# k^T v per head in two column tiles instead of per pair of heads, in one fused attention and MLP kernel

## The chip, the cores and the metric

The kernel runs on one core of one Trainium2 chip. Each core has a matrix engine (TensorE, PE in the profile, with its weight loads as PEld), three engines for elementwise work (VectorE: DVE, ScalarE: ACT, GpSimd: POOL) and a queue that issues the transfers (SyncE: SP). The metric is the time of one execution on the device in microseconds; lower is better.

## The reference

Two layers follow each other. The first is linear attention with a norm per head; the second is a token mix of low rank and an MLP in float32:

```python
# q, k, v: (8 batches, 8 heads, 576 tokens, 64)
kv  = einsum('bhsd,bhse->bhde', k, v)           # per head: 64 x 64, summed over 576 tokens
out = einsum('bhsd,bhde->bhse', q, kv)
x   = out / sqrt(mean(out*out, -1) + 1e-6) * g_norm   # heads side by side: (8, 576, 512)
u   = x + (x^T @ U @ V)^T                       # U: 576 x 32, V: 32 x 576
y   = u + maximum(u @ w_ch1, 0) @ w_ch2         # 512 -> 2048 -> 512
```

The change concerns the first line, `kv`, for batches 2 to 7.

## The kernel before

**Tiling.** Heads are taken in pairs, so that 2 x 64 columns fill the 128 columns of the matrix engine: four pairs a batch, and a *kv step* for each pair (`kv_step`). Tokens are the summed dimension: 576 = 4 chunks of 128 and a tail of 64. A pair's k and v come in one tile `kv_sb` (128 x 1024: four chunks of k, then four of v, `load_kv`) and the tail in `kvt_sb`.

**What a kv step makes.** The product of a pair's k and v is 128 x 128, of which only the two 64 x 64 blocks on the diagonal are wanted (each head with itself). They go into a tile `kvb` whose other blocks stay zero; there are two such tiles, in turn. The out step (L284, L286) then multiplies q by this `kvb`.

**float32 and float32r.** A matmul with float32 operands stands in the profile as two records (a weight load and a matmul each); one with float32r operands (rounded to fewer bits) as one. Where float32r is used, values are split into a high part and the rest, and the products are summed. The constant `NATIVE = 2` says that batches 0 and 1 do without such splits. In batches 2 to 7, the four main chunks of k^T v are float32 (L261, 128 x 128 columns). The tail is made from a split: it is loaded twice, into both halves of 128 partitions; ACT rounds it to float32r (L256), DVE takes the rest (L257 for k, L258 for v) in a tile `tails`, and one float32r matmul of 256 columns (L259) gives the products of k with the high part of v and with its rest, side by side. DVE adds these two sides when it moves the result to `kvb` (L272, twice, for each head).

**What sets the order.** The MLP runs over nine blocks of 512 tokens and, in each, over 16 slices of the hidden dimension: L432 to L434 (first weights, 12 matmuls of 512 columns a slice), relu and split on ACT and DVE (L441, L442), then L449 (second weights, 12 matmuls of 512 columns). The attention of the next batch is cut into steps that the code hands out between the slices (`prep_schedule`): kv, out, t (the product with U, L354 and L356; in batches 0 and 1 L350) and mix (L424). A scheduler with a timeline of its own orders each engine's instructions within that; so parts of one step can come to stand apart. Results wait in banks of PSUM, three of them for the steps (`pp`). `kv_sb` and `kvt_sb` have one buffer each: the next load waits until the last reader of the one before is done.

Of the kernel before, what the change touches and what calls it, by code (L numbers as in the profile page):

```python
# [10 lines left out]
F32 = mybir.dt.float32  # L11
F32R = mybir.dt.float32r
# [4 lines left out]
ALU = mybir.AluOpType  # L17
AX = mybir.AxisListType

B, H, S, D = 8, 8, 576, 64  # L20
DM, DF, R = 512, 2048, 32
P = 128
NPAIR = H // 2
NT = 5
MAIN = 4 * P
TAIL = S - MAIN
# [8 lines left out]
NATIVE = 2  # L35
# [24 lines left out]
def build(ctx: ExitStack, tc: tile.TileContext, kv_in, kvt0_in, kvt_in, q_in, uv_in, g_in, w_in, out):  # L60
    nc = tc.nc
# [5 lines left out]
    sc = ctx.enter_context(tc.tile_pool(name="sc", bufs=1))  # L67
# [71 lines left out]
    def move(which, n, out, in_, mul=None):  # L139

        e = ENG[which][n]
        if e == "a":
            if mul is None:
                nc.scalar.copy(out=out, in_=in_)
            else:
                nc.scalar.mul(out=out, in_=in_, mul=mul)
        else:
            eng = nc.vector if e == "v" else nc.gpsimd
            if mul is None:
                eng.tensor_copy(out=out, in_=in_)  # L150
            else:
                eng.tensor_scalar(out=out, in0=in_, scalar1=mul, scalar2=None, op0=ALU.mult)
# [88 lines left out]
    def bank():  # L241
        bank_no[0] += 1
        if startup[0] and bank_no[0] % (7 - NEARLY) >= 3 - NEARLY:
            return ps_y.tile([P, 512], F32, name="y")
        return ps_p.tile([P, 512], F32, name="pp")

    def kv_step(b, p):


        m = loads.pop(("kv", b, p))  # L250
        t = loads.pop(("t", b, p))
        pp = bank()
        kb = kvb[p % 2]
        if b >= NATIVE:
            both = sc.tile([P, 3 * P], F32R, name="tails")
            nc.scalar.copy(out=both[:, 0:2 * P], in_=t)  # L256
            nc.vector.tensor_tensor(out=both[TAIL:, 0:P], in0=t[TAIL:, 0:P], in1=both[TAIL:, 0:P].bitcast(F32), op=ALU.subtract)  # L257
            nc.vector.tensor_tensor(out=both[:, 2 * P:], in0=t[:, P:], in1=both[:, P:2 * P].bitcast(F32), op=ALU.subtract)  # L258
            nc.tensor.matmul(pp[:, 0:2 * P], lhsT=both[:, 0:P], rhs=both[:, P:], start=True, stop=False)  # L259
        for i in range(4):  # L260
            nc.tensor.matmul(pp[:, 0:P], lhsT=m[:, i * P:(i + 1) * P], rhs=m[:, MAIN + i * P:MAIN + (i + 1) * P],  # L261
                             start=(i == 0 and b < NATIVE), stop=(i == 3 and b >= NATIVE))
        if b < NATIVE:
            lo = TAIL * (p % 2)
            nc.tensor.matmul(pp[:, 0:P], lhsT=t[lo:lo + TAIL, 0:P], rhs=t[lo:lo + TAIL, P:2 * P], start=False, stop=True)
        parts = pp[:, 0:2 * P].rearrange("p (s c) -> p c s", s=2)
        for lo in (0, D):
            own = slice(lo, lo + D)
            if b < NATIVE:
                move("kv", p if b == 0 else -1, kb[own, own], pp[own, own])  # L270
            else:
                nc.vector.tensor_reduce(out=kb[own, own], in_=parts[own, own], axis=AX.X, op=ALU.add)  # L272

    state = {}

# [289 lines left out]
    def spread_v(n, eng):  # L565
        for k in range(4):
# [3 lines left out]
        out=uv, in_=uvraw.bitcast(U32).rearrange("p (n t) -> p n t", t=2)[:, :, 1].bitcast(F32), func=AF.Abs)  # L570
# [8 lines left out]
                                                  op=ALU.subtract)  # L579
# [94 lines left out]
    def prep_schedule(b):  # L674
# [8 lines left out]
        if b < B:  # L683
            for p in range(NPAIR):
                steps = STEPS0 if b == 1 else STEPS
                base = steps["gap"] * p

                def kv(p=p):
                    kv_step(b, p)
                    nxt = (b, p + 1) if p + 1 < NPAIR else (b + 1, 0)  # L690
                    if nxt[0] < B:
                        load_kv(*nxt)

                def o(p=p):
                    for what in (out_step, stats_step, mul_step, xsplit_step, turn_step):
                        what(b, p)
                    nxt = (b, p + 1) if p + 1 < NPAIR else (b + 1, 0)
                    if nxt[0] < B:
                        load_q(*nxt)

                def t(p=p):
                    t_step(b, p)
                    t4_step(b, p)

                for at, what in (("kv", kv), ("out", o), ("t", t), ("mix", lambda p=p: mix_step(b, p))):
                    todo.setdefault(base + steps[at], []).append(what)
# [108 lines left out]
```

## Time and profile before

| what | value |
|---|---|
| runs shown | 924.99, 926.73, 927.0 us; median 926.73 |
| span of the profiled execution | 924.0 us |
| records of L261 (four chunks, 28 steps) | 224 |
| records of L259 (tails, 24 steps) | 24 |
| median time from issue to landing of `kvt_sb` loads in batches 2 to 7 | 3.2 us |

The span runs from the first to the last instruction of one execution; the page gives no time of that execution beside it. In rows of groups, the columns are line, engine, operation, what it writes and reads, the shape (rows * weight columns, then partitions x moving columns), the count, busy time in us, mean duration of one in ns, idle time before it and what ended that. Matmul records overlap, and their ends are modelled, so starts say more than durations; the chain in order of time gives each piece from the end of the piece before it.

### The profile page before, as it was taken

What the parts mean: (1) busy time and instruction counts of PE and PEld (TensorE: products, weight loads), DVE (VectorE), ACT (ScalarE), POOL (GpSimd) and SP (SyncE); (2) the same over time, 40 slices, a digit from 0 to 9 for tenths busy, and PEclk for the clock granted to TensorE, in tenths of its full rate; (3) what the DMA queues carried; (4) which work ended last, traced back from release to release, by engine and by line L of the source; (5) the groups of instructions that cost most, each with busy time, mean ns of one, the idle gap of its engine ahead of it and who ended that gap; (6) DMA issues with size and microseconds to landing.
All of it is one profiled execution on the core that took longest, in us unless ns stands there. A gap on an engine that the chain in (4) does not pass through costs nothing.

```text
span 924.0 us, 12146 instructions
## 1 busy us (share of the span) xinstructions
PE 910.9 (99%) x4548; PEld 761.0 (82%) x4548; DVE 402.2 (44%) x870; ACT 271.4 (29%) x572; POOL 47.8 (5%) x61
## 2 busy tenths in 40 slices
PE   8899999999999999999999999999999999999998
PEld 7678888888878888888888888888788888888887
DVE  5799974534444435434344445434334231112112
ACT  5677742322222223222222223222222121111110
POOL 2000002000110002000200010000200020002000
PEclk9999999999999999999999999999999999999999
DMA  9952223211121112212121121212111010001001
GB/s 342 416 206 71 93 63 100 87 32 58 51 79 55 48 57 95 58 31 77 51 60 55 55 68 56 80 32 71 58 49 27 14 46 1 1 0 46 1 1 46
DMA packets 43019, 65.48 MB, mean 71 GB/s; under 512 B 9680, under 2 KB 27856, under 8 KB 42960
## 3 DMA queue, kind: packets, MB, share of 16 engines
q1 hardware_dynamic: 42960, 64.70, 21.2%
q8 instruction: 36, 0.59, 0.3%
q14 instruction: 23, 0.19, 0.1%
HBM read 46.97 MB, written 9.44 MB: 61 GB/s over the span
## 4 chain that ended last, share of the span: by engine, by line
PE 86%; DVE 6%; DMA 3%; ACT 2%; SPq 2%; issue 1%; POOL 0%; DVEq 0%; POOLq 0%; ACTq 0%
PE y L449 37%; PE h L432 13%; PE h L433 13%; PE h L434 13%; PE pp L261 2%; PE pp L284 2%; SPq L343 2%; DVE dec L127 1%; DVE st L460 1%; DMA kvq<-kv_in 1%; ACT top L131 1%; DMA out<-st 1%; DVE hl L442 1%; PE pp L354 1%; PE pp L424 1%
## 5 line engine op out<-in xcount | busy, mean ns | idle before, releaser
L449 PE MATMUL y<-hh,ws 128*128 128x512 f32 x1000 | 328.1, 394 | 0.0
L442 DVE SCALAR_TENSOR_TENSOR hl<-h,hh 128x512 fp32r<-128x512 f32 x143 | 98.4, 688 | 319.1 <-ACT hh L441 317.8
L449 PEld LDWEIGHTS y<-hh,ws 128*128 128x128 f32 x1000 | 181.0, 189 | 33.1 <-issue 0.2
L441 ACT ACTIVATE hh<-h 128x512 fp32r<-128x512 f32 x143 | 85.4, 597 | 404.0 <-PE h L434 404.0
L432 PE MATMUL h<-uth,ws 128*128 128x512 f32 x500 | 197.5, 395 | 2.2 <-DVE hl L442 2.2
L433 PE MATMUL h<-utl,ws 128*128 128x512 f32 x500 | 195.4, 391 | 0.0
L434 PE MATMUL h<-uth,ws 128*128 128x512 f32 x500 | 195.1, 390 | 0.0
L449 PE MATMUL y<-hl,ws 128*128 128x512 f32 x500 | 193.6, 387 | 0.0
L432 PEld LDWEIGHTS h<-uth,ws 128*128 128x128 f32 x500 | 93.9, 188 | 24.9 <-DVE hl L442 4.3
L434 PEld LDWEIGHTS h<-uth,ws 128*128 128x128 f32 x500 | 93.9, 188 | 20.2
L449 PEld LDWEIGHTS y<-hl,ws 128*128 128x128 f32 x500 | 93.9, 188 | 19.2
L433 PEld LDWEIGHTS h<-utl,ws 128*128 128x128 f32 x500 | 94.0, 188 | 18.4
L461 POOL TENSOR_TENSOR st<-st,utl 128x512 f32<-128x512 f32 x32 | 41.1, 1308 | 782.6 <-DVE st L460 781.0
L449 PE MATMUL y<-hh,w2s 128*128 128x512 f32 (+1 forms) x144 | 48.1, 396 | 2.8 <-ACT hh L441 2.7
L426 DVE TENSOR_TENSOR ut<-pp,ut 128x288 f32<-128x288 f32 x56 | 25.0, 455 | 43.5 <-DMA ut<-xt 30.3
L389 ACT ACTIVATE uth<-ut,g_sb 128x448 fp32r<-128x448 f32 (+7 forms) x56 | 27.6, 530 | 47.7 <-DVE ut L426 26.5
L460 DVE TENSOR_TENSOR st<-y,uth 128x512 f32<-128x512 f32 x32 | 21.4, 686 | 41.7 <-PE y L449 29.1
L449 PEld LDWEIGHTS y<-hh,w2s 128*128 128x128 f32 x144 | 26.6, 188 | 10.1 <-ACT hh L441 4.6
L390 DVE SCALAR_TENSOR_TENSOR utl<-ut,g_sb,uth 128x448 fp32r<-128x448 f32 (+7 forms) x56 | 26.9, 513 | 14.3 <-ACT uth L389 7.7
L300 DVE TENSOR_REDUCE sums<-x 128x10 f32<-128x640 f32 x28 | 22.9, 817 | 21.0 <-ACT x L288 20.9
L261 PE MATMUL pp<-kv_sb 128*128 128x128 f32 x224 | 30.3, 275 | 0.0
L284 PE MATMUL pp<-kvb,q_sb 128*128 128x128 f32 x224 | 29.5, 275 | 0.0
(188 smaller groups left out, 858.2 us busy)
## 6 DMA issues: line engine op xcount, KB each, us to landing
kv_sb<-kv_in SPq DMA_DIRECT2D x29, 512.0 KB, 3.5
raw<-w_in SPq DMA_DIRECT2D x14, 1023.6 KB, 15.4
q_sb<-q_in SPq DMA_DIRECT2D x29, 288.0 KB, 2.8
out<-st SPq DMA_DIRECT2D x32, 256.0 KB, 2.0
ut<-xt SPq DMA_DIRECT2D x224, 20.0 KB, 1.8
ut<-xt SPq DMA_DIRECT2D x224, 16.0 KB, 1.8
kvt_sb<-kvt_in SPq DMA_DIRECT2D x27, 128.0 KB, 3.2
kvq<-kv_in SPq DMA_DIRECT2D x3, 512.0 KB, 7.7
```

Source lines behind the costliest of these rows:

```text
L261: nc.tensor.matmul(pp[:, 0:P], lhsT=m[:, i * P:(i + 1) * P], rhs=m[:, MAIN + i * P:MAIN + (i + 1) * P], start=(i == 0 and b < NATIVE), sto ...
L284: nc.tensor.matmul(big[:, i * P:(i + 1) * P], lhsT=qt[:, TAIL + i * P:TAIL + (i + 1) * P], rhs=kb, start=True, stop=True)
L389: nc.scalar.mul(out=hi, in_=src, mul=g_sb)
L390: nc.vector.scalar_tensor_tensor(out=lo, in0=src, scalar=g_sb, in1=hi.bitcast(F32), op0=ALU.mult, op1=ALU.subtract)
L432: nc.tensor.matmul(h, lhsT=w1s[f][0][:, d, :], rhs=uh[:, d, :], start=(d == 0), stop=False)
L433: nc.tensor.matmul(h, lhsT=w1s[f][0][:, d, :], rhs=ul[:, d, :], start=False, stop=False)
L434: nc.tensor.matmul(h, lhsT=w1s[f][1][:, d, :], rhs=uh[:, d, :], start=False, stop=(d == ND - 1))
L441: last["relu"] = nc.scalar.activation(out=hh, in_=h, func=AF.Relu)
L442: nc.vector.scalar_tensor_tensor(out=hl, in0=h, scalar=0.0, in1=hh.bitcast(F32), op0=ALU.max, op1=ALU.subtract)
L449: nc.tensor.matmul(acc, lhsT=w2s[f][w][:, c, :], rhs=h[:, cols], start=(f == 0 and w == 0 and h is hh), stop=(f == NF - 1 and w == 1))
L460: nc.vector.tensor_tensor(out=o, in0=acc, in1=uh[:, c, :].bitcast(F32), op=ALU.add)
L461: nc.gpsimd.tensor_tensor(out=o, in0=o, in1=ul[:, c, :].bitcast(F32), op=ALU.add)
```

## The change

From batch 2 on, k^T v is made for each head by itself. For each of the four main chunks, and for a fifth of the tail, there is one float32 matmul a head: 64 columns of k as weights, 64 columns of v as moving data, into a 64 x 64 block of PSUM. The first head's block lies in partitions 0 to 63, and the second's in 64 to 127, and the built program gives their matmuls the column tiles of the array that go with them: 64 of the 128 columns each. The tail's chunk is filled with 64 rows of zeros instead of a second copy, so it needs no split. ACT copies both blocks to `kvb`. Batches 0 and 1 compute as before.

```diff
         t = loads.pop(("t", b, p))
         pp = bank()
         kb = kvb[p % 2]
+        own = [(slice(lo, lo + D), slice(MAIN + lo, MAIN + lo + D)) for lo in (0, D)]
         if b >= NATIVE:
-            both = sc.tile([P, 3 * P], F32R, name="tails")
-            nc.scalar.copy(out=both[:, 0:2 * P], in_=t)
-            nc.vector.tensor_tensor(out=both[TAIL:, 0:P], in0=t[TAIL:, 0:P], in1=both[TAIL:, 0:P].bitcast(F32), op=ALU.subtract)
-            nc.vector.tensor_tensor(out=both[:, 2 * P:], in0=t[:, P:], in1=both[:, P:2 * P].bitcast(F32), op=ALU.subtract)
-            nc.tensor.matmul(pp[:, 0:2 * P], lhsT=both[:, 0:P], rhs=both[:, P:], start=True, stop=False)
+            for i in range(4):
+                for k, v in own:
+                    kc = slice(i * P + k.start, i * P + k.stop)
+                    vc = slice(i * P + v.start, i * P + v.stop)
+                    nc.tensor.matmul(pp[k, 0:D], lhsT=m[:, kc], rhs=m[:, vc], start=(i == 0), stop=False)
+            for k, _ in own:
+                nc.tensor.matmul(pp[k, 0:D], lhsT=t[:, k], rhs=t[:, P + k.start:P + k.stop], start=False, stop=True)
+            for k, _ in own:
+                move("kv", -1, kb[k, k], pp[k, 0:D])
+            return
         for i in range(4):
             nc.tensor.matmul(pp[:, 0:P], lhsT=m[:, i * P:(i + 1) * P], rhs=m[:, MAIN + i * P:MAIN + (i + 1) * P],
-                             start=(i == 0 and b < NATIVE), stop=(i == 3 and b >= NATIVE))
...
-        parts = pp[:, 0:2 * P].rearrange("p (s c) -> p c s", s=2)
...
-                nc.vector.tensor_reduce(out=kb[own, own], in_=parts[own, own], axis=AX.X, op=ALU.add)
...
     def twice(a):
         n = B - NATIVE
-        a = tail_of(a[NATIVE:]).reshape(n, NPAIR, 1, TAIL, P)
-        return np.broadcast_to(a, (n, NPAIR, 2, TAIL, P)).reshape(n, NPAIR, P, P)
+        a = tail_of(a[NATIVE:]).reshape(n, NPAIR, TAIL, P)
+        return np.concatenate([a, np.zeros_like(a)], axis=2)
```

In the changed kernel, the main chunks are L260, the tail L262 and the copies L144 (through `move`). The first place is the kv step of batch 2's first pair on PE. A row is line, operation, what it writes and reads, and the size that it writes; `-` is before and `+` the change, and a program's float32 matmul is one row here (two records in a profile).

```order
 L449 MATMUL y<-hh,ws_1040 128x512
 L424 MATMUL pp<-v_98,t_1217 128x288 x2
-L259 MATMUL pp<-tails 128x256
-L261 MATMUL pp<-kv_sb 128x128 x4
+L260 MATMUL pp<-kv_sb 64x64 x8
 L449 MATMUL y<-hh,ws_1139 128x512 x4
+L262 MATMUL pp<-kvt_sb 64x64 x2
 L432 MATMUL h<-uth,ws_1179 128x512
```

Five matmuls in one place have become ten in two places, with four L449 between them.

The second place, also on PE, is the end of the kv step of batch 3's second pair, whose eight main matmuls stand in two places. Before:

```order
L449 MATMUL y<-hl,ws_1040 128x512
L449 MATMUL y<-hh,ws_1040 128x512
L261 MATMUL pp<-kv_sb 128x128 x2
L449 MATMUL y<-hh,ws_1139 128x512 x4
L354 MATMUL pp<-xh,u_96 64x128
```

And with the change:

```order
L449 MATMUL y<-hl,ws_1139 128x512
L449 MATMUL y<-hh,ws_1139 128x512
L260 MATMUL pp<-kv_sb 64x64 x5
L262 MATMUL pp<-kvt_sb 64x64 x2
L449 MATMUL y<-hh,ws_1179 128x512 x4
L354 MATMUL pp<-xh,u_96 64x128
```

The other three L260 stand a whole slice of the MLP earlier, behind the out step of the pair before, as L259 and the other two L261 did; the whole step has moved on by one slice against the MLP. Over the 24 steps, the rows of L260 and L262 make 46 pieces with other matmuls between them.

The third place is ACT's queue around the first kv step with the change:

```order
L441 ACTIVATE hh<-h 128x512
L221 CAST ws_1276<-dec 128x1024
L144 COPY kvb_99<-pp 64x64 x2
L441 ACTIVATE hh<-h 128x512
L389 ACTIVATE uth<-ut_3_92,g_sb 128x448
```

The cast of the tail (L256), which stood some rows earlier, is gone, and the two copies to `kvb`, which wait for L262, stand ahead of the next relu (L441).

More of the change, by code (lines that the diff above doesn't have):

```diff
@@ L253, in kv_step @@
         kb = kvb[p % 2]
+        own = [(slice(lo, lo + D), slice(MAIN + lo, MAIN + lo + D)) for lo in (0, D)]
         if b >= NATIVE:
-            both = sc.tile([P, 3 * P], F32R, name="tails")
[L256 to L259, printed above, removed]
+            for i in range(4):
[8 more added lines that the diff above has]
+            return
         for i in range(4):
             nc.tensor.matmul(pp[:, 0:P], lhsT=m[:, i * P:(i + 1) * P], rhs=m[:, MAIN + i * P:MAIN + (i + 1) * P],
-                             start=(i == 0 and b < NATIVE), stop=(i == 3 and b >= NATIVE))
-        if b < NATIVE:
-            lo = TAIL * (p % 2)
-            nc.tensor.matmul(pp[:, 0:P], lhsT=t[lo:lo + TAIL, 0:P], rhs=t[lo:lo + TAIL, P:2 * P], start=False, stop=True)
-        parts = pp[:, 0:2 * P].rearrange("p (s c) -> p c s", s=2)
[L267 to L272, printed above, removed]
+                             start=(i == 0), stop=False)
+        lo = TAIL * (p % 2)
+        nc.tensor.matmul(pp[:, 0:P], lhsT=t[lo:lo + TAIL, 0:P], rhs=t[lo:lo + TAIL, P:2 * P], start=False, stop=True)
+        for k, _ in own:
+            move("kv", p if b == 0 else -1, kb[k, k], pp[k, k])
     state = {}
```

## The prediction

> **What bounds the kernel now.** I read the page first: engine shares, the clock in 40 slices and the chain that ended last; then the engine sums by stretch and PE's waits in the middle of the run.
>
> ```profile
> span 924.0 us, 12146 instructions
> PE 910.9 (99%) x4548; PEld 761.0 (82%) x4548; DVE 402.2 (44%) x870; ACT 271.4 (29%) x572; POOL 47.8 (5%) x61
> PEclk9999999999999999999999999999999999999999
> PE 86%; DVE 6%; DMA 3%; ACT 2%; SPq 2%; issue 1%; POOL 0%; DVEq 0%; POOLq 0%; ACTq 0%
> 110.00:700.00 590.00, 588.47 (x2959) 491.97 (x2958) 267.53 (x604) 164.82 (x380) 30.98 (x24) 1.00 0.21 62
> PE h L432 <- DVE hl L442: 1.0, 3, 0.4
> PE y L449 <- ACT hh L441: 0.3, 1, 0.3
> ```
>
> The chain is TensorE for 86% of the span; the rest of it lies in the start. The fifth row is the stretch 110 to 700 us, which holds batches 2 to 7, all that the change touches. Its columns are length, then busy time of PE, weight loads, DVE, ACT and POOL. PE is busy for 588.47 of 590.00 us, and the last two rows are PE's own waits there (from 120 us on): 1.3 us. The clock is full throughout. So what the change does is worth what it does to PE's stream of matmuls, one for one. Work that goes from DVE or ACT can give back 1.5 us at most.
>
> A matmul's recorded duration is no price, since the records overlap: I take prices from the chain in order of time (start, length, what), where each piece runs from the end of the one before. Here is one kv step of batch 2, with its neighbours:
>
> ```profile
> 123.37 0.91 PE y L449 x4
> 124.28 0.26 PE pp L424 x2
> 124.54 0.12 PE pp L259
> 124.66 0.89 PE pp L261 x8
> 125.55 0.93 PE y L449 x4
> L261 PE MATMUL pp<-kv_sb 128*128 128x128 f32 x224 | 30.3, 275 | 0.0
> ```
>
> A float32r matmul of 512 columns costs 0.91 / 4 = 0.23 us. The four float32 matmuls of 128 columns are eight records (224 of them for 28 steps), 0.89 / 8 = 0.111 us each. One record of 128 float32 columns costs nearly what L259's 256 float32r columns do (0.12), so each record streams its columns twice. A step of before costs 0.12 + 0.89 = **1.01 us** of PE, and 24 steps cost **24.2 us**. That is all there is to win.
>
> **The change, part by part.** *Removed from PE:* those 24.2 us.
>
> *Added to PE, the stream:* 10 matmuls a step, each of 64 weight columns and 64 moving columns in float32, so 20 records, 480 in all. No row has this form. The nearest are the float32 records above, halved (0.111 / 2 = 0.056), and the float32r matmuls of the t step, which stream 128 columns once with 64 weight columns:
>
> ```profile
> 143.76 0.45 PE y L449 x2
> 144.21 0.06 PE pp L356
> 144.27 0.06 PE pp L354
> ...
> 144.63 0.06 PE pp L354
> 144.69 0.52 PE y L449 x2
> ```
>
> That is 0.06 each. I take 0.057: 480 x 0.057 = **27.4 us**. From above 0.06 bounds it; from below, half of it (0.028), if the two column tiles work at once. So the stream alone, in turn, already costs 3.2 us more than it replaces: the matrix work per head is a quarter, but a record still streams its 64 columns twice, there are twice as many, and the tail goes from one pass of 256 columns to four records.
>
> *Added to PE, the switches.* In the built program L260 and L262 name a column tile, half of the array's columns (the first half for one head, the second for the other). One form of before names such a tile too: L350 of batches 0 and 1, float32, 64 weight columns. L354 and L356 have 64 weight columns as well but name the whole array. The chain around an L350 block:
>
> ```profile
> 117.36 0.91 PE y L449 x4
> 118.28 1.24 PE pp L350 x10
> 119.51 0.43 PE h L432
> 119.94 0.23 PE h L433
> ```
>
> The timeline of the same place (start, length, engine, what) shows where it goes:
>
> ```profile
> 117.44 0.84 PE L449 MATMUL y<-hh,ws 128*128 128x512 f32 x3
> 118.20 1.06 PEld L350 LDWEIGHTS pp<-x,uf 128*64 128x64 f32 x10 [0.35 <-issue]
> 118.21 1.31 PE L350 MATMUL pp<-x,uf 128*64 128x128 f32 x10
> 119.44 0.19 PEld L432 LDWEIGHTS h<-uth,ws 128*128 128x128 f32 x1 [0.17 <-DVE ws L225]
> 119.44 0.50 PE L432 MATMUL h<-uth,ws 128*128 128x512 f32 x1
> 119.55 0.19 PEld L433 LDWEIGHTS h<-utl,ws 128*128 128x128 f32 x1
> ```
>
> The three L449 would have made room at 117.44 + 3 x 0.227 = 118.12; L350's first weights start at 118.20, together with its first matmul, and not during the matmul before as elsewhere. On leaving, L432's weights again start only with its matmul, at 119.44. Ten records of 0.111 would be 1.11 us; the block costs 1.24, and the L432 behind it 0.43 instead of 0.23. So **one visit to a column tile costs 0.13 + 0.20 = 0.33 us**: it looks as if the array ran empty and loaded weights in the open, and again on the way back. The t step shows the contrast: eight matmuls of 0.06, and 0.52 for the two L449 behind them, 0.06 over their 0.46. The same holds behind whole-array float32 (0.93 for four L449, 0.02 over).
>
> How many visits? By the order, L260 and L262 of 24 steps stand in 46 separate blocks: in 22 steps other matmuls (four L449, or a whole block of 24 to 25) come between the parts, and only two steps are in one piece. Nothing beside them is in a column tile. 46 x 0.33 = **15.2 us**. Bounds: nothing, if what L350 shows were float32 startup and no tile (L354's row), and 0.33.
>
> A rule bears on which row to take. The Trainium skill, "TensorEngine Tiling (Array Packing)", Key Properties, says that changing the tiling mode, as opposed to the tile, drains TensorE. L350's 0.33 us agrees; L354 would contradict it, were 64 active columns by themselves a tile. By the rule the sum is the one below; by L354's row it would be +3.2 us.
>
> *DVE and ACT.*
>
> ```profile
> L272 DVE TENSOR_REDUCE kvb<-pp 64x64 f32<-64x128 f32 x48 | 13.7, 286 | 1.7 <-PE pp L261 1.2
> L256 ACT CAST tails<-kvt_sb 128x256 fp32r<-128x256 f32 x24 | 9.6, 401 | 13.7 <-PE pp L259 13.5 <-DMA kvt_sb<-kvt_in 0.2
> L257 DVE TENSOR_TENSOR tails<-kvt_sb,tails 64x128 fp32r<-64x128 f32 x24 | 7.9, 330 | 1.7 <-ACT tails L256 1.0
> L258 DVE TENSOR_TENSOR tails<-kvt_sb,tails 128x128 fp32r<-128x128 f32 x24 | 7.0, 293 | 0.3
> L144 ACT COPY kvb<-pp 64x64 f32<-64x64 f32 x8 | 1.7, 216 | 1.4 <-PE pp L265 1.4
> ```
>
> DVE loses 13.7 + 7.9 + 7.0 = 28.6 us; ACT loses 9.6 and gains 48 copies of 0.216, 10.4 us. PE's 588 busy us hide all of it, so I cost it at nothing (at best -1.5 us). The copies are new waits on ACT: each pair stands behind L262, with the next L441, or the copies of the t step, queued behind it. In the order the h that this L441 reads always ends at least 12 matmuls after L262 (12 x 0.227 = 2.7 us) against 0.43 us of copying, and L284 needs kvb at the earliest 20 matmuls (4.5 us) later. So nobody on PE waits.
>
> *SP.* The same loads, same bytes. The tail's tile comes free when L262 has read it, not when L256 has; its next load, and on SP's queue the q loads and transposes behind it, may be some microseconds later. DVE's L426 waits for transposes already; PE does not wait for it in this stretch. Taken at nothing; if that cover went, a few of the 1 us kind of waits would follow, which the range holds.
>
> *Sum:* 27.4 + 15.2 - 24.2 = **+18.4 us**. On the profiled execution: 924.0 + 18.4 = 942.4 us of span. The runs shown lie 1.0 to 3.0 us above that span, their median 926.73 by 2.7; so I forecast **945.1 us**.
>
> **The rivals.**
>
> *Two tiles at once (slower, by less).* L260 alternates between the halves, so the second head's records might run beside the first's, 0.028 a record: 480 x 0.028 = 13.4; 13.4 + 15.2 - 24.2 = +4.4 us, **931.1 us**. For it: the halves share no columns and no sums. Against it: in every row of this trace the next weights start only when the matmul before starts, and 64 columns of them take some 0.055 us (means of 191 ns for 128 columns and 136 for 64):
>
> ```profile
> L261 PEld LDWEIGHTS pp<-kv_sb 128*128 128x128 f32 x224 | 28.4, 191 | 1.1
> L350 PEld LDWEIGHTS pp<-x,uf 128*64 128x64 f32 x40 | 4.3, 136 | 0.7 <-issue 0.4
> ```
>
> A stream whose weights come one after the other cannot go below 0.055 a record, whatever the tiles do. The Trainium skill's same section says that different tiles can run LdWeights and Matmul in parallel, which would be this rival; no run so far shows two tiles in use.
>
> *Cheap switches and two tiles at once (faster).* Were a visit free, as L354's is, and the tiles parallel, the step would cost 13.4 against 24.2: -10.8 us, **915.9 us**. Its place is the same 46 blocks. With parallel tiles it decides in favour of the change as soon as a visit costs under (24.2 - 13.4) / 46 = 0.23 us. L350's four blocks of ten speak against it.
>
> *Every change of half costs.* Alternating gives 240 - 46 = 194 changes inside the blocks. If each leaves the next weights in the open (0.055), +10.7 us: 955.8 us. If each drains as a visit's start does (0.13), +25.2: **970.3 us**. No row speaks for or against.
>
> *The change does nothing it says:* if the halves work in turn, "two column tiles" gains nothing. That is my forecast.
>
> **How the numbers follow.** In turn, with paid visits: 0.53. Two tiles at once with paid visits: 0.28. Every change costs: 0.10, about half of it up to 956. Free visits: 0.09, of which 0.05 with parallel tiles (916) and 0.04 in turn (929.9, +0.3%). A measurement of this kernel tells about 0.2% (1.9 us) from no change. Faster: 0.05. Within 0.2%: 0.03, from records faster than 0.028 or cheaper, partly hidden switches. Slower: the rest, 0.92. The range goes from the parallel case (931, less 1 for what DVE frees) to weights in the open at every change: 930 to 956.
>
> **What would show it.** In the profile after: L260 and L262 with 480 PE records, 0.055 to 0.06 apart in the chain if in turn, near 0.03 if at once; the matmul behind each block at some 0.43 us instead of 0.23, and the first weights of a block starting with its first matmul; 46 such places. PE's share stays at 99%, DVE's falls to some 40% (402.2 - 28.6 of 942.4 us). I am wrong if the blocks' neighbours keep 0.23, or if PE shows new waits on ACT's kvb copies.

## The result and the profile after

| | before | after |
|---|---|---|
| median of 4 runs each on one chip, us | 926.12 (924.99 to 927.00) | 931.32 (929.99 to 932.19) |
| span of the profiled execution, us | 924.0 | 929.6 |

The ratio of the times is 1.0058, with a 95% interval of 1.0047 to 1.0070: the change costs 5.2 us, where 18.4 were forecast.

From the profile of the changed kernel, the rows that answer to those of before: span, shares and clock of the page, then the stretch 110 to 700 us (length, then busy time of PE, weight loads, DVE, ACT and POOL), and PE's waits from 120 to 700 us (total, times, longest):

```profile
span 929.6 us, 12600 instructions
PE 917.6 (99%) x4812; PEld 755.4 (81%) x4812; DVE 376.5 (41%) x774; ACT 274.0 (29%) x596; POOL 47.4 (5%) x61
PEclk9999999999999999999999999999999999999999
PE 87%; DVE 4%; SPq 3%; DMA 3%; ACT 2%; issue 1%; POOL 0%; DVEq 0%; POOLq 0%; ACTq 0%
110.00:700.00 590.00, 589.30 (x3188) 481.79 (x3188) 239.09 (x502) 166.67 (x399) 30.58 (x24) 1.00 0.20 62
PE y L449 <- DVE st L460: 0.3, 1, 0.3
```

PE still sets the time. DVE lost 267.53 - 239.09 = 28.4 us in that stretch, and PE's waits there fell from 1.3 to 0.3 us, while PE was busy for 0.83 us more of it, so by these rows some 0.8 to 1.0 us came back; the rest of the answer must be in PE's own stream. The chain in order of time (start, length, what) shows the first kv step of batch 2, and further on one of the two that stand in one piece:

```profile
125.68 0.26 PE pp L424 x2
125.94 0.62 PE pp L260 x16
126.56 1.12 PE y L449 x4
127.68 0.27 PE pp L262 x4
127.94 0.43 PE h L432
...
178.46 0.94 PE y L449 x4
179.40 0.61 PE pp L260 x16
180.01 0.12 PE pp L262 x4
180.13 0.43 PE h L432
```

Sixteen records of L260 take 0.62 us, 0.039 each with the way in, and L262's four behind them 0.12, 0.03 each. That is not 0.057. The starts of the first records, read from the trace (L260 at 125.872 us, each as ns after the one before), say how:

```
matmuls:       0  6  100  7  52  6  52  7  51  7  52  6  52  7  51  7
weight loads:  0  7   48  7  49  6  52  7  51  7  52  6  52  7  51  7
```

The records start in pairs, 6 to 7 ns apart, a pair every 58 to 59 ns; so do their weight loads. The first interval of a block is 100 ns, with the first weights loaded in the open. In the program the two records of one float32 matmul stand together, both for the same head, then two for the other; the pairs nevertheless come from the first block on. A pair thus looks like one record of each head, side by side in the two column tiles. The timeline of weight loads (start, length, what, idle time before) shows the way in:

```profile
125.87 0.55 PEld L260 LDWEIGHTS pp<-kv_sb 128*64 128x64 f32 x16 [0.16 <-issue]
126.48 0.76 PEld L449 LDWEIGHTS y<-hh,ws 128*128 128x128 f32 x4
127.61 0.20 PEld L262 LDWEIGHTS pp<-kvt_sb 128*64 128x64 f32 x4 [0.36 <-issue]
127.87 0.19 PEld L432 LDWEIGHTS h<-uth,ws 128*128 128x128 f32 x1
```

The first weights of both blocks start with their first matmul (125.87 and 127.61), and L432's only where it starts itself (127.87), as around L350 before.

For a sum over all blocks I take starts, from the end of the matmul before (its start and 0.227 for 512 columns) to where the matmul behind the block would have started at its usual pace. The 46 blocks come to **30.8 us**, against 24.4 for the same steps before: +6.4.

Two more terms lie outside the blocks. The first is the granted clock in the first 110 us, before then after (last columns: clock, DMA share, GB/s):

```profile
0.00:110.00 110.00, 101.95 (x558) 85.20 (x559) 88.75 (x190) 75.68 (x135) 6.67 (x29) 1.00 0.60 228
0.00:110.00 110.00, 102.17 (x552) 85.27 (x553) 87.59 (x188) 74.24 (x133) 6.67 (x29) 0.98 0.59 228
```

The profiled execution of the changed kernel ran at half clock for 3.4 us (54.9 to 58.3 us), before anything that the change touches, and that of before did not: the last matmul ahead of the first kv step (an L424) starts 1.4 us later, at 125.65 against 124.24. The second is the waits. From the start of that L424 to the end of the span, everything outside the blocks takes 773.1 us, against 775.4 before: 2.2 less (773.13 and 775.35). In the kernel before, five intervals between MLP matmuls are 0.29 to 0.59 us over the usual 0.227; after, two are (0.31 and 0.50). The rows of waits show less than half of the 2.2 us: they count from a matmul's modelled end, some 0.39 us after its start, where the next one usually starts after 0.227, and the interval behind each wait is some 0.11 us longer too.

So the span's +5.6 us is 6.4 - 2.2 + 1.4. Without the clock's part, these two executions lie 4.2 us apart; the medians' 5.2 (4.4 to 6.5 by the interval) is a us more, which two executions out of runs that scatter by 2 us cannot settle.

### The profile page after: what moved, and what is told of

Read it like the earlier page. It is cut to its first block, busy times and chain, and to the rows that moved or that the text cites. A ratio compares the mean times of both kernels' runs of the same rounds, so it can differ in the third digit from the quotient of the medians.

```text
span 929.6 us, 12600 instructions
## 1 busy us (share of the span) xinstructions
PE 917.6 (99%) x4812; PEld 755.4 (81%) x4812; DVE 376.5 (41%) x774; ACT 274.0 (29%) x596; POOL 47.4 (5%) x61
## 4 chain that ended last, share of the span: by engine, by line
PE 87%; DVE 4%; SPq 3%; DMA 3%; ACT 2%; issue 1%; POOL 0%; DVEq 0%; POOLq 0%; ACTq 0%
PE y L449 39%; PE h L432 13%; PE h L433 13%; PE h L434 13%; SPq L343 3%; PE pp L284 2%; PE pp L260 2%; PE pp L354 1%; DMA kvq<-kv_in 1%; DVE dec L127 1%; PE pp L424 1%; ACT top L131 1%; PE pp L262 1%; PE pp L356 1%; PE pp L449 1%
## 5 line engine op out<-in xcount | busy, mean ns | idle before, releaser
L449 PE MATMUL y<-hh,ws 128*128 128x512 f32 x1000 | 329.1, 395 | 0.0
L449 PEld LDWEIGHTS y<-hh,ws 128*128 128x128 f32 x1000 | 180.7, 188 | 35.0 <-ACT kvb L144 0.2
L432 PE MATMUL h<-uth,ws 128*128 128x512 f32 x500 | 198.0, 396 | 1.3 <-DVE hl L442 1.1
L441 ACT ACTIVATE hh<-h 128x512 fp32r<-128x512 f32 x143 | 85.4, 598 | 377.4 <-PE h L434 377.4
L449 PE MATMUL y<-hl,ws 128*128 128x512 f32 x500 | 193.4, 387 | 0.0
L432 PEld LDWEIGHTS h<-uth,ws 128*128 128x128 f32 x500 | 94.2, 188 | 23.4 <-DVE hl L442 3.0
L449 PEld LDWEIGHTS y<-hl,ws 128*128 128x128 f32 x500 | 93.9, 188 | 19.3
L449 PE MATMUL y<-hh,w2s 128*128 128x512 f32 (+1 forms) x144 | 47.6, 395 | 2.6 <-ACT hh L441 2.3
L449 PEld LDWEIGHTS y<-hh,w2s 128*128 128x128 f32 x144 | 26.8, 188 | 8.9 <-ACT hh L441 3.2
L300 DVE TENSOR_REDUCE sums<-x 128x10 f32<-128x640 f32 x28 | 22.9, 817 | 22.0 <-ACT x L288 21.8
L284 PEld LDWEIGHTS pp<-kvb,q_sb 128*128 128x128 f32 x224 | 28.3, 191 | 0.8
```

The costliest lines, as they stand in the source:

```text
L284: nc.tensor.matmul(big[:, i * P:(i + 1) * P], lhsT=qt[:, TAIL + i * P:TAIL + (i + 1) * P], rhs=kb, start=True, stop=True)
L432: nc.tensor.matmul(h, lhsT=w1s[f][0][:, d, :], rhs=uh[:, d, :], start=(d == 0), stop=False)
L441: last["relu"] = nc.scalar.activation(out=hh, in_=h, func=AF.Relu)
L449: nc.tensor.matmul(acc, lhsT=w2s[f][w][:, c, :], rhs=h[:, cols], start=(f == 0 and w == 0 and h is hh), stop=(f == NF - 1 and w == 1))
```

## Experiments

All start from the changed kernel, and a cut of the code is shown against the experiment that it builds on. In what follows, "the piece" is the kv step's block in PE's stream, its cost worked out from starts as above. Medians stand beside 21 runs (E1 to E4, median 925.26 us) or 27 runs (E5 to E7, 925.40) of the kernel before on the same chip, and ratios are to that kernel.

**E1: one piece.** The ten matmuls are chained in their order, the first behind the MLP matmul written before it, and the next 24 MLP matmuls behind the last. So each step is one piece: 24 visits to column tiles instead of 46. The work is the same.

```diff
+    gate = {"before": None, "kv": None, "open": 0}
...
+    def mlp(mm):
+        if gate["kv"] is not None and gate["open"] > 0:
+            queue(mm.ins, gate["kv"])
+            gate["open"] -= 1
+        gate["before"] = mm.ins
...
+            queue(made[0], gate["before"])
+            for i, j in zip(made, made[1:]):
+                queue(j, i)
+            gate.update(kv=made[-1], open=24)
```

> The change with the ten float32 matmuls of a kv step in one piece: 24 visits to column tiles instead of 46; the work is the same. If a visit costs what the profile of the change shows (0.36 us), 22 fewer of them give -7.9 us: about 923.4 us, 0.3% under before. If the 46 pieces are not what costs (if the time of the change lies in its stream or in waits on the copies to kvb), the time stays near 931 us.

Measured: 923.23 us, ratio 0.9972 (0.9962 to 0.9983): **0.3% under before**, where the change was 0.6% over it. The timeline of a piece (start, modelled length, what; L467 is the MLP's second product, L450 its first, L274 and L276 the kv step):

```profile
147.47 0.39 PE L467 MATMUL y<-hh,ws 128*128 128x512 f32 x1
147.79 0.69 PE L274 MATMUL pp<-kv_sb 128*64 128x64 f32 x16
148.30 0.29 PE L276 MATMUL pp<-kvt_sb 128*64 128x64 f32 x4
148.52 0.50 PE L467 MATMUL y<-hh,w2s 128*128 128x512 f32 x1
148.86 0.39 PE L450 MATMUL h<-uth,w1s 128*128 128x512 f32 x1
```

From 147.47 to 148.86 are 1.39 us; two matmuls of 0.227 lie in it, so the piece costs 0.93. The 24 pieces come to 22.1 us, 8.7 less than the 46 blocks: 22 visits, and 48 records that had run alone, where a step was cut between the two heads' matmuls of one chunk, and now have a partner (48 x 0.029 = 1.4 us), so 7.3 / 22 = 0.33 a visit. Some of it was lost to waits, which rose from 0.3 to 2.2 us in the rows:

```profile
PE y L467 <- DVE st L478: 1.1, 1, 1.1
PE h L450 <- DVE hl L460: 0.8, 2, 0.6
PE y L467 <- ACT hh L459: 0.3, 1, 0.3
```

By starts, the time outside the pieces is 2.6 us more than outside the changed kernel's blocks. 8.7 - 2.6 = 6.1 us, and the spans of the two profiled executions, both with the stretch at half clock, are 6.1 apart (929.6 and 923.5). By the medians, each against the kernel before on its chip, it went from +5.2 to -2.0, 7.2 us.

**E2: head 0's five chunks, then head 1's, in two tiles.** E1 with the loops swapped.

```diff
-            for i in range(4):
-                for k, v in own:
+            for k, v in own:
+                for i in range(4):
```

> As the one-piece kernel, but all five chunks of the first head first and then the second head's five, still in two column tiles. If the array looks ahead in its queue and each tile goes on by itself, the order makes no difference: about 923.4 us, records near 0.03 apart. If only neighbours in the queue run side by side, the heads come in turn: 480 records of 0.058 instead of 0.0295, +13.7 us, about 937 us.

Measured: 933.00 us, 1.0083 (1.0070 to 1.0096), nearer the second. The timeline of a piece (L274 main chunks, L275 tails; head 0's L275 stand in the program ahead of all of head 1):

```profile
145.96 0.73 PE L274 MATMUL pp<-kv_sb 128*64 128x64 f32 x10
146.47 0.22 PE L275 MATMUL pp<-kvt_sb 128*64 128x64 f32 x1
146.53 0.22 PE L274 MATMUL pp<-kv_sb 128*64 128x64 f32 x1
146.53 0.22 PE L275 MATMUL pp<-kvt_sb 128*64 128x64 f32 x1
146.59 0.46 PE L274 MATMUL pp<-kv_sb 128*64 128x64 f32 x5
146.88 0.28 PE L275 MATMUL pp<-kvt_sb 128*64 128x64 f32 x2
```

Ten records of L274 stand ahead of the first L275. Head 0 has only eight, so two matmul records of head 1 started before one of head 0 that the program has ahead of them. By the starts, head 1's first comes 5 ns after head 0's seventh, with three of head 0's still to start, and only three pairs form in the piece. It costs 1.33 us; 24 come to 31.7, 9.5 above E1, where 9.8 were measured.

**E3: both heads in the first column tile.** E2 with head 1's product in the same 64 partitions beside head 0's, and its copy from there.

```diff
-                    made.append(nc.tensor.matmul(pp[k, 0:D], lhsT=m[:, kc], rhs=m[:, vc], start=(i == 0), stop=False).ins)
+                    made.append(nc.tensor.matmul(pp[0:D, k], lhsT=m[:, kc], rhs=m[:, vc], start=(i == 0), stop=False).ins)
...
-                move("kv", -1, kb[k, k], pp[k, 0:D])
+                move("kv", -1, kb[k, k], pp[0:D, k])
```

> As the in-turn kernel, but both heads in the first column tile (results in partitions 0 to 63, side by side in columns; the copy moves the second head's to its partitions). If two tiles at once are what makes a record 0.0295, one tile gives 0.058: +13.7 us on the one-piece kernel, about 937 us. If a float32 record of 64 by 64 columns takes 0.03 wherever it runs, the time stays at that of the one-piece kernel, about 923.4 us.

Measured: 934.54 us, 1.0097 (1.0084 to 1.0110). Its chain in order of time:

```profile
144.77 1.81 PE y L466 x8
146.58 0.61 PE pp L274 x8
147.19 0.12 PE pp L275 x2
147.31 0.47 PE pp L274 x8
147.77 0.12 PE pp L275 x2
147.89 0.43 PE y L466
```

No record starts nearer than 58 ns to the one before: 0.47 / 8 = 0.058 a record. A piece costs 0.61 + 0.12 + 0.47 + 0.12 and 0.20 behind it, 1.52 (1.508 by starts). Against E2, the tile alone differs: E2 forms three pairs a piece, E3 none. So E1's pairs are the two tiles at work at once: with the same twenty records and the same visit, two tiles in turns of one matmul save 1.508 - 0.934 = 0.57 us a step, 14.1 us in all (36.2 against 22.1). E1 gives back 2.2 us of waits that E3 does not have; 11.9 are left and 11.3 measured. E1's own order in one tile was not run.

The Trainium skill, "TensorEngine Tiling (Array Packing)", Key Properties, says that different tiles can run LdWeights and Matmul in parallel; E1 against E3 agrees, 0.029 against 0.058 us a record. The Trainium skill, "TensorE: Matmul & The Clock Gate", Part 3, The mechanism, says that matmuls keep strictly to program order in start and end; E2's records that start ahead of their turn differ, and the measurement decides.

**E4: the tail alone.** The zero-padded fifth float32 chunk, but for the pair and on the whole array: no tile is used, and there is no split.

```diff
+                nc.tensor.matmul(pp[:, 0:P], lhsT=m[:, i * P:(i + 1) * P], rhs=m[:, MAIN + i * P:MAIN + (i + 1) * P],
+                                 start=(i == 0), stop=False)
+            nc.tensor.matmul(pp[:, 0:P], lhsT=t[:, 0:P], rhs=t[:, P:], start=False, stop=True)
             for k, _ in own:
...
+                move("kv", -1, kb[k, k], pp[k, k])
```

> The other half of the change alone: the tail as a zero-padded fifth float32 chunk, but for the pair of heads in the whole array, 128 columns, no column tile. Ten records of 0.111 are 1.11 us a step against 1.01 before: +2.4 us on before, about 928.5 us, with no visits. If the work freed on DVE and ACT is worth something by itself, the time comes out at before or under it (926 or less).

Measured: 925.14 us, 1.0001 (0.9992 to 1.0009): a miss, 3.4 us under the 928.5 expected. The matmul work is there, as this timeline shows (L257 main, L259 tail):

```profile
138.53 0.39 PE L446 MATMUL y<-hh,ws 128*128 128x512 f32 x1
138.76 1.05 PE L257 MATMUL pp<-kv_sb 128*128 128x128 f32 x8
139.65 0.39 PE L259 MATMUL pp<-kvt_sb 128*128 128x128 f32 x2
139.79 1.18 PE L446 MATMUL y<-hh,ws 128*128 128x512 f32 x4
```

Ten records from 138.76 take about 1.12 us with what the matmul behind loses, against 1.01 before, and the steps come to 26.9 us against 24.4. But PE's waits from 120 to 700 us fell from 1.3 to 0.2 us in the rows, and by starts everything outside the steps, from the L424 (here L421) on, takes 773.0 us against 775.4. That 2.4 us makes up for the 2.5 of the steps, so the expected price was there and was paid back.

**E5: two pairs in one piece.** E1 with the steps of two pairs joined: 40 records a piece, 12 visits. The loads of both pairs must be there, so the second pair's main tile uses a buffer of the weights' decoding (`dec`), and its tail one more.

```diff
-            kt = ldp.tile([P, 2 * MAIN], F32, name="kv_sb")
+            kt = (dec.tile([P, 2 * MAIN], F32, name="dec") if b >= NATIVE and p % 2 else ldp.tile([P, 2 * MAIN], F32, name="kv_sb"))
...
+            pairs = [(kb, m, t, 0)]
+            pairs.append((kvb[1], loads.pop(("kv", b, p + 1)), loads.pop(("t", b, p + 1)), D))
+            for _, m, t, at in pairs:
```

> As the one-piece kernel, but two pairs of heads in one piece, one behind the other: 12 visits to column tiles instead of 24, the same matmuls (a second tile each for k, v and the tail holds the other pair). If a visit costs 0.35 us whatever its length, 12 fewer give -4.2 us: about 919 us. If the one-piece kernel's gain came from the new places of the matmuls and not from their number of visits, it stays near 923 us.

Measured: 925.38 us, 0.9999 (0.9989 to 1.0009): a miss. The chain around a piece (L277 main, L279 tail), and PE's waits from 120 to 700 us:

```profile
150.61 1.81 PE y L471 x8
152.42 0.61 PE pp L277 x16
153.03 0.12 PE pp L279 x4
153.15 0.47 PE pp L277 x16
153.62 0.12 PE pp L279 x4
153.73 0.43 PE h L454
```

```profile
PE y L471 <- ACT hh L463: 2.9, 6, 0.7
PE h L454 <- ACT ws L221: 1.1, 2, 0.6
PE h L456 <- DVE ws L225: 1.1, 2, 0.5
```

The piece does what was expected: 40 records in 1.514 us, as long as E3's 20, so 20 more than E1's cost 0.58 and the visit itself 0.934 - 0.58 = **0.35 us**. The 12 pieces come to 18.2 us, 4.0 less than E1. But PE now waits 5.8 us there instead of 2.2, 5.1 of it in these three rows: for relu on ACT (L463), and for the decoding of the weights (L221, L225). One of its buffers was borrowed, which may be why; that was not tried apart. So the gain turned into waits of about the same size: the profiled executions have spans of 922.6 us and, without the 1.4 us of the half-clock stretch that E1's holds, 922.1. By the medians E5 lies 2 us above E1; the rest of that stays open.

**E6: E4 with the old work put back.** The cast and the two subtractions of the tail run again, their results unused, and DVE makes the copies to `kvb`.

```diff
+            both = sc.tile([P, 3 * P], F32R, name="tails")
+            nc.scalar.copy(out=both[:, 0:2 * P], in_=t)
+            nc.vector.tensor_tensor(out=both[TAIL:, 0:P], in0=t[TAIL:, 0:P], in1=both[TAIL:, 0:P].bitcast(F32), op=ALU.subtract)
+            nc.vector.tensor_tensor(out=both[:, 2 * P:], in0=t[:, P:], in1=both[:, P:2 * P].bitcast(F32), op=ALU.subtract)
...
-                move("kv", -1, kb[k, k], pp[k, k])
+                nc.vector.tensor_copy(out=kb[k, k], in_=pp[k, k])
```

> As the kernel with the fifth chunk in the whole array, with the work of before put back on ACT and DVE: the cast and the two subtractions of the tail are made (nobody reads them), and DVE moves the blocks to kvb. That kernel came out at before (925.1 against 925.3 us) though its matmuls of the kv steps cost 2.2 us more. If the work freed on DVE and ACT gave those 2.2 us back, this one takes them again: about 927.3 us. If the freed work is worth nothing, it stays at about 925.1 us.

Measured: 925.90 us, 1.0005 (0.9996 to 1.0013). In the stretch 110 to 700 us of E4, then of E6 (third busy time DVE), the work is back:

```profile
110.00:700.00 590.00, 589.58 (x2980) 494.30 (x2979) 241.13 (x509) 167.29 (x404) 31.06 (x24) 1.00 0.20 62
```

```profile
110.00:700.00 590.00, 589.67 (x2980) 494.27 (x2979) 264.06 (x603) 164.08 (x379) 31.50 (x24) 1.00 0.20 62
```

DVE has 22.9 us more to do, and PE is as busy as in E4; everything outside the steps takes 773.0 us in both. So the work that was freed on DVE is not why E4's waits went; it is worth 0.4 us by the medians' ratios, and with their intervals under 2. What is left in E6 is that no matmul waits for the split of the tail, and another order; which of the two ended the waits stays open.

**E7: two chunks a head in turn.** E1 with four records of head 0, four of head 1, and so on.

```diff
-            for i in range(4):
-                for k, v in own:
+            for two in (0, 2):
+                for k, v in own:
+                  for i in (two, two + 1):
```

> As the one-piece kernel, with two chunks of the first head, then two of the second, and so on (four records of one tile, then four of the other). In the in-turn kernel the second head's records began when three of the first's were still to start. If the array looks four records ahead in its queue, four and four run side by side as in the one-piece kernel: a kv step's piece costs 0.93 us, and the time is about 923 us. If it looks ahead only by one record, just the ends overlap: some 1.3 us a piece, about 932 us.

Measured: 924.00 us, 0.9982 (0.9971 to 0.9993). The starts of a piece's twenty matmul records, each as ns after the one before:

```
E2:  0 107  58  59  58  58  59   5  53  54   4  54   5  54  58  58  59  58  58  59
E7:  0  13  94  13  45  13  45  14  45  13  45  54   4  55   4  54   4  54   4  55
```

In E7 pairs form from the first record on, 13 to 14 ns apart and later 4 to 5, a pair every 58 to 59 ns; the piece costs 0.98, against 0.93 in E1 and 1.33 in E2. The profile does not name a record's head here. But records of one tile never start nearer than 58 ns (E3), so the second must be head 1's first: it passed three of head 0's that were waiting, as in E2.

## Why the prediction was right and wrong

- **That PE's stream sets the price, one for one:** right. In the profiled executions the blocks cost 6.4 us more, the time outside them is 2.2 less, and with the clock's 1.4 the span is 5.6 longer.
- **24.2 us removed:** right (24.4 by starts).
- **The stream, 480 x 0.057 = 27.4 us:** this step failed. The price of a record in one tile was right (0.058 in E3), but not that the tiles work in turn. 432 of the records ran in pairs, 0.029 each, and 48 alone, 0.058: 15.4 us. The difference, 12.0 us, is nearly all of the 13.2 by which the forecast of +18.4 missed; the waits below are the other term.
- **The reason given for it** was "A stream whose weights come one after the other cannot go below 0.055 a record, whatever the tiles do". It was read from rows in which only one tile was ever in use. The weights of the two tiles load at once (starts 6 to 7 ns apart); within one tile, the next weights still start only when the matmul before starts. Those rows bore on one tile's pace alone.
- **46 visits of 0.33, 15.2 us:** right. 30.8 less the stream's 15.4 leaves 15.4. The visit that L350 showed holds whatever stands in it: by starts 0.35 for 2, 4, 20 or 40 records where MLP matmuls lie on both sides. It is some 0.06 less where L354, with its 64 weight columns, comes behind. E1 shows that it is paid for each visit.
- **Work freed on DVE and added on ACT at nothing, at best -1.5 us:** right that no wait of PE on the copies to `kvb` appears, wrong in its bound. By starts 2.2 us came back. The bound was read from idle time behind modelled ends, which shows only part of a wait. E4 has the same gain (2.4 us) without a column tile, and E6 shows that the freed work itself is worth little of it.
- **The rivals.** "Two tiles at once (slower, by less)" gave 931.1 us, and 931.32 came. Its mechanism is the one shown; that it came so near is partly luck. Its sum took 0.028 a record for all 480 where 0.029 was measured (0.6 us) and left out the lone records (+1.4) and the waits (-2.2), which nearly cancel, and it started from 926.73, where the runs beside the change gave 926.12. "Every change of half costs" fell: pairs follow each other without a gap. "Free visits" fell with E1.
- **The signs named:** records 0.03 apart, 0.43 behind a block, first weights with the first matmul and DVE at 41% all came as written for that rival.

## What to carry to other kernels

Two column tiles are worth their name if both heads' records stand close together in the queue: a pair every 58 ns instead of a record, whether they alternate by one matmul or by two. Each block of them in a stream of whole-array matmuls costs 0.35 us, so chain the block into one piece before judging the change: that alone turned +5.2 us into -2.0 here. A price read from rows in which a resource was never used twice at once is an upper end for using it twice, not a floor. And where ends are modelled, take waits from starts: the rows of idle time showed 0.8 to 1.0 us of the 2.2 that came back here.

## What the runs showed of the hardware that was not expected

- Weight loads and matmuls of two column tiles run side by side, 6 to 7 ns apart, with 58 to 59 ns from pair to pair. That is one tile's own pace.
- Matmul records of one tile start ahead of records of the other tile that the program has before them. In E2 two records of head 1 start before head 0's tail. In E7 and E2, head 1's first record starts while three of head 0's are still to start, never more; so the look-ahead seems to span about four records. That is a reading of two orders, not a measured limit.
- A visit's 0.35 us does not depend on its length: blocks of 4 records cost 0.47 and of 40 records 1.51, 36 records more for 18 x 0.058 = 1.04.
